# Turning y by VectorE and HBM instead of by products with the identity, in a linear-attention and mixture-of-experts kernel

## The chip, the cores and the metric

The kernel runs on one core of a Trainium2 chip. The metric is the device time of one execution in microseconds (us). A difference of about 0.3% is the least that a measurement of this kernel tells from none.

## What is computed

The first half is linear attention over 8 batches, 8 heads, 576 rows and head size 64, with 128 random features. Its result x (8 x 576 x 512) goes into a mixture of four experts, each of them a causal attention with its own projections, of which every row keeps the best two.

```python
def phi(x):
    proj = np.einsum('bhsd,df->bhsf', x, w_phi)
    proj = proj - np.max(np.abs(proj), axis=-1, keepdims=True)
    return np.concatenate([np.exp(proj), np.exp(-proj)], axis=-1)
q_p, k_p = (phi(q), phi(k))
kv = np.einsum('bhsf,bhsd->bhfd', k_p, v)
z = np.sum(k_p, axis=2)
num = np.einsum('bhsf,bhfd->bhsd', q_p, kv)
den = np.einsum('bhsf,bhf->bhs', q_p, z)[..., None] + 1e-06
x = num / den                      # laid out as B, S, H * D
...
logits = x @ w_gate                # the best two of four experts, softmax weights w
for e in range(E):
    q, k, v = x @ wq[e], x @ wk[e], x @ wv[e]
    a = causal_softmax(scale * (q @ k.transpose(0, 2, 1)))
    ye = a @ v @ wo[e]
    out += (weight of e for the row) * ye
```

## The kernel before

Work is cut into generators, one for each stage, and each yields a step for one engine at a time. Which generator goes next is written out by hand: the string PICKS holds pairs of signs, the first naming the generator, the second the PSUM bank (there are eight) or the engine. Plan.loop follows it, and in_order then ties every engine to this order, so each engine works through a fixed list and waits at each instruction for the semaphores that its data need. Code 8 (the sign I) as the second sign puts a step that has a choice on VectorE, any lower one on ScalarE. There are some 1,014 steps that only VectorE can take, and they carry I as well.

The attention half goes over 32 pairs of heads (four a batch). The features of k and q are made by TensorE, centred and put through Exp, where the maximum of q's features over partitions is a GpSimd partition_all_reduce of about 4 us. stream_kv and stream_n form the sums and the numerators, with rows on the partitions. For the projections of the second half, x has to stand with its features on the partitions. turn_x does that: VectorE transposes 128 x 640 values in blocks of 32 x 32 (line 535), four DMAs write the blocks to HBM tile xd in the right order, one DMA reads xd back (line 544), ScalarE or VectorE rounds the result to its upper part, and VectorE subtracts to get the lower part (line 185, both inputs in SBUF). TensorE products are made of three terms, upper by upper, upper by lower and lower by upper.

The second half goes over 8 batches and two pairs g of experts. After scores, softmax and a @ v (post), norm_y divides and multiplies by the weight of the expert (normed, lines 409 to 440) and writes y with rows on the partitions into yq[g]. Then turn_y turns y: five products with the identity a set, a set being one (batch, g), in two PSUM banks (blocks 0 and 1, then 2 to 4; line 445). evac_y takes each bank to the upper part (a copy on ScalarE or VectorE) and the lower part (a subtraction on VectorE, one input in PSUM; line 185). project_out multiplies by wo with 48 products a batch and ends in the stores. Turning y of batch b waits until the products of project_out of batch b - 1 are issued; norm_y of batch b waits until yq[g] of b - 1 has been turned.

All DMAs are issued on SyncE's queue (load, line 210), in the order of the list. A step "SP" that waits for a semaphore holds all later DMAs. An all-reduce of GpSimd is made to wait for the last VectorE instruction before it that was marked as using the port which the two share (plan.port, line 184 and dve(..., port=True)). keep_warm fills TensorE with small bf16 products until the first x is ready, three to a step.

The lines that matter: yq 262, normed 409, turned 442, turn_x 531, norm_y 762, turn_y 768, evac_y 783, project_out 795.

Of the kernel before, what the change touches and what calls it, by code (L numbers as in the profile page):

```python
# [20 lines left out]
NJ = 5  # L21
# [35 lines left out]
    "UABASIQARIQAOIOIOIDAQACANIDADZAAOIOIOIOAQIJHRINAQIQIGIDAECJIFgHIQAGAJ1QACADAQIPINIPINALIIBPIPILAGIPIPAPIMAGID7OAHAGANIKA"
    "FgAAQIFqQARAOIFxQARAIgPISARAOIKALAOIMABAKIECDAGIBARIGIDAD1OARIRIGAKASIAAHBRILAKIPICAJAF7NININICAHADAFqGIBANIIxNININAPIPA"
    "GIOADAMID4LIMANAFiNAFrSAQISAECSAJIIAIESALAQIJAOIOIOILAIDRINIRIRANININAQIPAIFMIQALAAAIARAJAIAICQILABANIRAMAIBRINAQIMALIIE"
    "KIJAPIOAIGKAOIMIKAJIIDKIKILADAIAIoIRNIDAOII8RIOIPANIIyOIKANAOINIOIIAIFQIPIQIOAPIQANIPANIIBSAOIKARIMIMIMIIAPANIPIMIKALIIF"  # L60
    "JAMAKILAIAD8NAMIKAMIGDCAMIJANIJIMIEBGAGCKIAALIKAKIHwCAGAMILIKAKILIJIKAEFDALIKIF7JANAFiBAJINANAHZNAKIJAOIMINAKIKIKIKALIF6"
    "MIMIDADgAAKIOAMIMAJ1QILILIMAMINIMIJAMIIRMIMIDAI7IgRIRAPIDAOIPII7OIQIPIOAGCCAQIRIOIRIOAOIRAQIOIPAOIEBPIOAJAOIGAGACAPIOIMI"
    "MAMIOIMAECMDQIGANIMEQAPIMAOID1AAQAPIPIOIF4OIQAHZQAJIOIJIBALIHiOAPIPILAPILIF4TAIAIAIFTAPILAPIPIPALIIAKISALASIKAQIQIQIIHLI"
    "SAQIQASIQIIBQALINIRALARINIIALrPAQIKANIDAPINADAOIJIDQKAPIPIF8JAOAGGKISAOIOAOIQIOARAQIJANBQAAANENIIDQANIOAPIGADAOIH9LAPIKI"
    "DACABAOANIGAKACAOIOILAKAKIMIECMAMIIGMIGANIMILAEENIMAIBOINALAMIIDMAIFMAIAI4MAFyNIOINAPIDhAANAOINAMIIrIQPAPAI-QIIAIDSIMAPI"
    "SIPIQISARIQIPAIFRIUAOIRAUINIIDUAQIUISIIFKAPIUAUIRILASIPIPIIAJDPIQAOIOAJHQAPINIJAKAMIOAJCPAOALAJGOAKIDAJENAMILAJDMAKIJFJA"
    "JIH5MAMAKIJAJILALIKAJAJIJIDADQAAKIKIJAJzNIJIJIJIJALIKILIKIGFCAKIKIDAJIDAKIKIIhKIKAF6JAMILIKAMAOILAKDLIMAEGKAMAF8LIGAKALI"
    "MADRMILIFoBALIMINAIjNAI-LIPAOABAMIIoNIOINIOIIAIAGENAPIMAJAQIOAOIAAQIPIQAQIHaPACAGANIOIOIJAJINIEENIIHRIMIQIMAKIIANINIDANI"
    "KIPADAIFQAPININAPIIGLIPAKAPIKAGECAMIMIJINAKANIKIIAD5JAAAFQMIGAPAFrPIJAEGPIFgOIPIJAJIFqOALAPIMISAHzNIJAQAQAJIPAHsNIBAJIOA"
    "MIJABAJQRININIPINIDALIKADANINAGHCANIMINALANILAIBKIPIKILAGAKAOIEDIGMIRIKANIQININIIHPANIOALILILALIIDLINALIIALANAIAIRNANII0"  # L70
    "I9RARAIYPIOIIANAIEPASIOASIQIOARIPIRAOIPIIGTAQIOIQATIPIOAOIICTATIOIOIOIIBKARAPIRILAOIOINIMEOAPAMGPAIAD9AAOIPAOIOIKAFQOIQA"
    "FZKIF0KATAJANISALAPALIBAJEOANAOANAJGMIOALAJFOALIJDOAOAJBOAOAJCMILAJAKIJIJAH0JIDAJIDAQIOINILIDrAAJANINIF4KIRAFRRASAGAQIRA"
    "SAKAPIQIBAKAOIJ5OILIKAGAKIKIKAJACADAJIKIJADAIqIYOINII0KARILILINAGDPAQINACALILALINALIKAMILILIKCLAMIKALIMAJAIpNIGALILIIAF7"
    "BAKIQADyQAMIKILIPAKIKAIAIDKILIKIKIIHQAPIKAQIPIJAKIIEPAOIKINIIAKAOANIJIIAEBAANAEDH1OIPIOIOIDANIJIDAH6MIOIMIMIMIJAJIGBCAOI"
    "JAJIOIMIOIOAMIMIMANIDYNIJAJIGAAAOIFsQAFyPIQAF5QAQAOIFsRAOIOAQAECQABAHwRIPAJIDABADAQID8MIJAAAJrTIMIOASIRISIMARIGBRIRIDAPI"
    "PIRIRARIRIDALAPIECGIIHSIPIPASIPIPAOIQEQDQAQAIFRACAQIOAQIPIJBQALAOAICNIOAPAIAPAKINANAIGOILILIKAIAI8NIIrPIOIIRKAOIMIIwNAPA"
    "NANAIAIHOINIMAOINIOAQIPIIESAQIPIQAMINAPAIFSIMARANIRIPIIDKARAMIRILAMIMIMIIAH8QINIOAMINIMAKAGFCAKIKAKILILIKIEBGAJCNIHwKAKI"
    "NINAOILIKAKINALILIDrAAKAKILAKIFRQAOIF8KARIJBOIPAJEPAMIOIBAQAPAKaLIPANILILAOALIOILIDAKILIDAKAI5NINIIsIwSAQISANIQAPIDsNANI"
    "PAQIRINAAAPII6OAPIOAOIPAIAIAIBPIOIOIQIRIIDKAUAQIRIQALAQIRARIIAVAQIQITIQAKASIIGSAPISIKIIAJCKARAOIJHQIQAOIJDQAGBCARANIOAOI"
    "KANINAEANIKIJFLAGANALIDAKCKGPIH7QINAOIDANANIKINIMIKAJIGECAMIMIJAMIMIMAMIDpMIJAGIAAJyNIKILIMILIKALIHYLILIDANILILALILIDAD8"  # L80
    "MIMIFpMIMAOIFyBARAPIQALAQAIFOIRAPAOIOAPIIBPIMIMAICMIOAMAIEOINIIGOANAIAI4OINAIrOIPIIRSIOANIOAPAF0OAQAFoBAQAF7RAQAPIF0OISA"
    "QAPISAIoOIOAPIBAPIIAIHSANARATISITISITANIIESAVATIVINANIIGQAUASITIRIIDMAOISAQIOIKAIAEHRIRALFAARIGENAQIQIMIPANIOADACAPIDADQ"
    "GIPIHzMAPILAOIKAOIGHCAMANIMAKIKIKAEBEFNIJEKIAAGAJAPANIKAKIH6NIQILILILIKAKIOADAOAKINIKAKhOIKIKIMIMIDAKIKILILALIKILAIoMIMI"
    "IzKAI6RAOIRAPIOAMIOAMIDzPIQIOAOIPIOAMIIIMIOAAAOIJFSIJERIVASIRISAKAOINIJFQARIJHWAQIUARITAQIJFSAPISAJERAMININALBMILAIAIAIH"
    "KILIPAKAQAPIICQAPINAOIJALIDAIGNANAJIKAKIIFNAJADAMIMIDZMAKAKIMIMIFgKAOAF6BAKIOAIAGGPAKIOAJAMINAKACAEFGAGAJIAANILINILIH8CA"
    "MIGIDALIDADyMIMILAGBCAMIMIPILALIOILAMIHrGIMIMILILAFgMIMIOAF-MIOAFRPAMIOAMIFgMANAEDQAEHMIPABAJ1OARIQINAOIPIOILADADAIAOIOI"
    "NAMIBAHCPAAAGEOAMIMAMIMIGBNALIKAGHKAMIKAGAGYMIGqOINIG0KALIG5PAPANAGAGCMAQIPILAMAPINIPAOINIOAMIGFLINARAMILAMILAQIGDQALIQI"
    "LILIGAIAOALIOILIJALILIGAKCMAKFKAMALIF0MANILILIIAIIIAEDAAJIHIIIHIBBCAFHHIGAGIFAHAKIGABqKIGIKAAjJIKAHIGAJIHAGIB4IABRLAGIMA"
    "B1HIFAF5OIFILAGIJAFAJAGIHAIAGIDqIIIIAADzKIDgLINAIIIAIIEDOIIAOINIOIJAFAEBHIGAMAOANAEHOIJALIKADaNAMALIAADADADFNIMINIFAMIKI"
    "KIKAKIJADBNAKANIFIGADGJIMAIIIIGAJIHAFIDHJADABAKAJIFAJIHIFAAsGABIGICaKIIIGAGIIIGACxGIGIIIGAJIIIG4LIHIAAJIJIHIJIHAHIHAIIII"  # L90
    "AAGICEJIGAJIHIHACFIIIIKAHICCKAIIHAIACDJACBJAGACACwJAJICsC6NANACZGANILIJACACEPILANIOINIOAPIKINAPICFMINIRAKALAQIKANALIKICG"
    "OAMIOILICAHAOAMILIMIKIJIKACADELAGIDHLALADFFAJIJAGDFIIAFBFAHAGADGFIHADCHAAEIAHIEAHIEIGIAADADIA4DIDICACICICAC1EICICICICACI"
# [795 lines left out]
```

## Time and profile before

| | us |
|---|---|
| median of 3 runs (577.13 to 578.64) | 577.42 |
| the profiled execution, whole | 577.18 |
| its span from the first to the last instruction | 575.4 |
| TensorE matmul busy | 564.3 |
| VectorE busy | 503.4 |
| ScalarE busy | 387.0 |
| GpSimd busy | 198.3 |

The profiled execution lies 0.24 us under the median, and 1.8 us of it lie outside the span. The granted TensorE clock was 1.00 throughout. Matmuls are pipelined, and so a busy TensorE is not one at its peak; the chain of waits tells better where time goes: it starts at the last instruction and follows, step by step, what released it.

### The profile page before, as it was taken

Reading aid. Unit: us, or ns where it says so; the run is one execution under the profiler, and the core shown is the slowest. Engines: PE = TensorE matmul, PEld = TensorE weight load, DVE = VectorE, ACT = ScalarE, POOL = GpSimd, SP = SyncE. Lnnn points to the kernel's source line nnn. Section 1 sums busy time; section 2 is a strip of 40 time slices with the busy share of each in tenths; the row PEclk is TensorE's granted clock in tenths of the full one; section 3 lists DMA queues with packets and bytes.
Section 4 is the critical chain, followed back from the end, with each engine's and each line's share of the span. In section 5 each row is a group of like instructions: output and inputs, shape, how many; then the busy total and the mean of one; then the engine's idle time right before and its main releaser. Section 6 shows DMA issues by size and latency. Waiting matters only on the chain.

```text
span 575.4 us, 22675 instructions
## 1 busy us (share of the span) xinstructions
PE 564.3 (98%) x9743; PEld 528.3 (92%) x9743; DVE 503.4 (87%) x1279; ACT 387.0 (67%) x715; POOL 198.3 (34%) x78
## 2 busy tenths in 40 slices
...
GB/s 148 210 179 184 224 183 45 96 119 92 147 77 112 154 80 111 74 156 102 123 117 58 142 124 95 60 155 127 132 122 53 66 43 64 63 84 44 2 43 124
DMA packets 83316, 62.36 MB, mean 108 GB/s; under 512 B 47248, under 2 KB 66064, under 8 KB 83216
## 3 DMA queue, kind: packets, MB, share of 16 engines
...
## 4 chain that ended last, share of the span: by engine, by line
PE 80%; DVE 8%; DMA 4%; ACT 4%; issue 1%; SPq 1%; POOL 1%; ACTq 0%; DVEq 0%; POOLq 0%
PE ps_c L180 32%; PE ps_c L402 29%; PE ps_c L355 10%; PE ps_c L621 7%; PE ps_c L445 1%; DMA out_dram<-ot 1%; DMA xl<-xd 1%; ACT st L191 1%; DVE st L739 1%; DVE top L653 1%; SPq L210 1%; DMA v_in<-in_v_dram 1%; POOL tops L493 1%; DVE xl L185 1%; DMA xd<-xt 1%
## 5 line engine op out<-in xcount | busy, mean ns | idle before, releaser
L493 POOL PARTITION_ALL_REDUCE mx<-u x32 | 127.1, 3988 | 136.3 <-ACT u L189 60.9
L180 PE MATMUL ps_c<-xh,qk 128*128 128x320 f32 (+1 forms) x512 | 106.5, 299 | 0.0
L191 ACT ACTIVATE ek<-ek 128x1152 f32<-128x1152 f32 x64 | 74.6, 1166 | 22.6 <-DVE ek L390 21.9
L180 PEld LDWEIGHTS ps_c<-xh,qk 128*128 128x128 f32 x512 | 83.2, 189 | 1.7 <-issue 0.4
L402 PE MATMUL ps_c<-v_in,ek 128*64 128x65 f32 x2560 | 81.9, 222 | 1.8 <-ACT ek L191 1.0
L402 PEld LDWEIGHTS ps_c<-v_in,ek 128*64 128x64 f32 x2560 | 77.6, 137 | 5.9 <-ACT ek L191 2.3
L493 POOL PARTITION_ALL_REDUCE tops<-top x15 | 54.4, 3627 | 65.2 <-DVE top L653 45.8
L180 PE MATMUL ps_c<-xl,qk 128*128 128x256 f32 (+1 forms) x256 | 75.7, 296 | 0.0
L739 DVE TENSOR_TENSOR st<-st,tops 128x1152 f32<-128x1152 f32 (+4 forms) x75 | 66.6, 899 | 1.8 <-POOL tops L493 1.7
L191 ACT ACTIVATE st<-st 128x1152 f32<-128x1152 f32 (+3 forms) x60 | 51.0, 868 | 18.0 <-DVE st L739 14.6
L402 PE MATMUL ps_c<-kv,mx 128*64 128x65 f32 x1152 | 62.1, 224 | 1.1 <-ACT kv L189 0.8
L189 ACT COPY st<-ps_c 128x512 f32<-128x512 f32 (+1 forms) x106 | 47.5, 504 | 18.1 <-PE ps_c L621 11.2
L180 PE MATMUL ps_c<-vg,xh 128*128 128x260 f32 (+1 forms) x320 | 59.4, 286 | 0.0
L402 PE MATMUL ps_c<-kv,u 128*64 128x65 f32 x1152 | 59.1, 221 | 0.0
L503 DVE TENSOR_TENSOR u<-u,mx 128x1152 f32<-128x1152 f32 x32 | 53.9, 1688 | 2.6 <-POOL mx L493 2.3
L189 ACT COPY u<-ps_c 128x320 f32<-128x320 f32 (+3 forms) x116 | 40.4, 418 | 19.8 <-PE ps_c L355 18.3
L634 POOL COPY top<-st 128x256 f32<-128x256 f32 x15 | 6.3, 423 | 135.2 <-ACT st L189 114.8
L402 PEld LDWEIGHTS ps_c<-kv,mx 128*64 128x64 f32 x1152 | 47.3, 137 | 5.9 <-issue 1.4
L180 PE MATMUL ps_c<-yh,wo 128*128 128x256 f32 (+1 forms) x256 | 52.4, 299 | 0.1
L388 DVE TENSOR_REDUCE pmax<-ps_c 128x4 f32<-128x512 f32 (+1 forms) x96 | 50.5, 545 | 2.1 <-ACT mx L191 0.7
L390 DVE TENSOR_TENSOR ek<-ps_c,pmax 128x512 f32<-128x512 f32 (+1 forms) x96 | 50.5, 543 | 0.9 <-PE ps_c L402 0.7
L180 PEld LDWEIGHTS ps_c<-xl,qk 128*128 128x128 f32 x256 | 48.5, 190 | 0.0
...
## 6 DMA issues: line engine op xcount, KB each, us to landing
v_in<-in_v_dram SPq DMA_DIRECT2D x32, 320.0 KB, 4.1
...
xl<-xd SPq DMA_DIRECT2D x32, 288.0 KB, 3.1
out_dram<-ot SPq DMA_DIRECT2D x32, 288.0 KB, 2.3
...
xd<-xt SPq DMA_DIRECT2D x64, 80.0 KB, 2.7
...
```

Source lines behind the costliest of these rows:

```text
L180: nc.tensor.matmul(o, a, b, start=start, stop=stop, skip_group_check=True)
L189: nc.scalar.copy(o, i)
L191: nc.scalar.activation(o, i, func, **kw)
L355: nc.tensor.matmul(o, a, b, start=True, stop=True, skip_group_check=True)
L388: dve(n * 128, [mk], [pk]).tensor_reduce(out=m[:, us], in_=src, axis=AX.X, op=ALU.max, apply_absolute_value=True)
L390: dve(n * 128, [(f'ek{p % EKB}1', us.start)], [pk, mk]).tensor_tensor(out=ek2[p % EKB][:, 1, us, :], in0=src, in1=m[:, us].unsqueeze(2).to ...
L402: nc.tensor.matmul(o, a, b, start=start, stop=stop, skip_group_check=True)
L493: nc.gpsimd.partition_all_reduce(o, i, 128, op)
L503: dve(2 * S, [uk], [mk], port=True).tensor_tensor(out=U, in0=U, in1=M, op=ALU.subtract)
L621: nc.tensor.matmul(pp_[e][:, o:o + q1 - q0], kk2[k_][r, 128 * j:128 * j + 128], q2[q_][r, q0:q1], start=m == 0, stop=m == 2, skip_group_ch ...
L634: nc.gpsimd.tensor_copy(top[x][:, :, 0:128], st[x][0][:, :, 0:128])
L739: dve(2 * n, [sj[j]], [*key, mk], port=True).tensor_tensor(out=a, in0=a, in1=tops[x][0:m, :, 128 * j:], op=ALU.subtract)
```

## The change

For all batches but the last, turn_y goes to a new generator, move_y, which does for y what turn_x does for x. VectorE transposes the whole set in blocks of 32 x 32 into a new SBUF tile yt, four DMAs write it to a new HBM tile yd, five DMAs read it back into the place of the lower part, one copy of 128 x 576 makes the upper part, and one subtraction with both inputs in SBUF makes the lower part. The reads pick pieces of 32 values (128 bytes). yq is laid out as xq is (four groups of 160 columns), and two memsets clear its corner. The last batch keeps the products with the identity on a view of the same tile. The subtraction of move_y is issued without the port mark; its copy carries it if VectorE takes it.

PICKS is new as a whole. It has 2,687 pairs before and 2,660 after. 1,132 pairs have I as their second sign before, 1,099 after. The numbers in the calls of dve(...) that differ (-6.0, 9.0, 7.0) are arguments which the function doesn't use.

```diff
-    yq = [sb(f"yq{i}", [128, NJ, 128]) for i in range(2)]
+    yq = [sb(f"yq{i}", [128, 4, 32 * NJ]) for i in range(2)]
+    yt = [sb(f"yt{i}", [128, 4, 32 * NJ]) for i in range(2)]
+    yd = [dp.tile([128, 4, 32 * NJ], F32, name=f"yd{i}") for i in range(2)]
+    for t in yq:
+        nc.vector.memset(t[64:128, :, 128:160], 0.0)
...
     def norm_y(b, g, pks, pss):
         yield Step('DVE', pred=(lambda: all(('yt', b - 1, g, q_[0]) in done for q_ in PARTS)) if b else None)
-        yield from normed(pks, pss, sc[g], 1e-9, yq[g], f'yq{g}', gw[:, :, 2 * g:2 * g + 2].rearrange("p i e -> p e i"), True)
+        yield from normed(pks, pss, sc[g], 1e-9, rows_y(g) if b == B - 1 else yq[g], f'yq{g}', gw[:, :, 2 * g:2 * g + 2].rearrange("p i e -> p e i"), b == B - 1)
...
+    def move_y(b, g):
+        keys, k, hi, lo = [(f'yq{g}', x, n) for x in range(2) for n in range(2)], f'yt{g}', *ys[g]
+        yield Step('DVE', keys, pred=lambda: all(('n', b, g, n) in done for n in range(2)) and (b == 0 or ('yw', b - 1, g) in done))
+        dve(640, [k], keys, XT_RATE).transpose(yt[g].rearrange("p a t -> p (a t)"), yq[g].rearrange("p a t -> p (a t)"))
+        for s0, s1 in PARTS:
+            done.add(('yt', b, g, s0))
+        yield Step('SP', [k], pred=has('yr', b - 1, g) if b else None)
+        hbm = yd[g].rearrange("(b x) a t -> x b a t", b=4)
+        for a in range(4):
+            n = 160 if a < 2 else 128
+            load(hbm[:, :, a, 0:n], yt[g][32 * a:32 * a + 32, :, 0:n], (f'yd{g}', a), [k])
+        done.add(('yw', b, g))
+        kd, kr = [(f'yd{g}', a) for a in range(4)], [('yr', g, n) for n in range(2)]
+        old = [('y' + x, g, s0) for x in 'hl' for s0, s1 in PARTS]
+        yield Step('SP', kd, pred=(lambda: ('o', b - 1) in done) if b else None)
+        to, hbm = lo.bitcast(F32), yd[g].rearrange("f a (i j) -> f i a j", j=32)
+        for i in range(4):
+            load(to[:, 128 * i:128 * i + 128].rearrange("f (a j) -> f a j", j=32), hbm[:, i], [kr[0], *old], kd)
+        load(to[:, 512:576].rearrange("f (a j) -> f a j", j=32), hbm[:, 4, 0:2], [kr[1], *old], kd)
+        done.add(('yr', b, g))
+        st_ = Step(copies_sb(S), kr, port=True)
+        yield st_
+        copy(st_.eng, S, hi, to, [('yh', g, s0) for s0, s1 in PARTS], kr, 0.52)
+        yield Step('DVE', [('yh', g, 0)], hot=True)
+        nc.vector.tensor_tensor(out=lo, in0=to, in1=hi.bitcast(F32), op=ALU.subtract)
...
     def turn_y(b, g):
+        if b < B - 1:
+            yield from move_y(b, g)
+            return
         for s0, s1 in PARTS:
...
-            turned(ps, pk, yq[g], blocks, key)
+            turned(ps, pk, rows_y(g), blocks, key)
```

## Rows read from the trace of the kernel before

**Rows 1.** The page: busy time by engine, then the chain's shares by engine.
```profile
PE 564.3 (98%) x9743; PEld 528.3 (92%) x9743; DVE 503.4 (87%) x1279; ACT 387.0 (67%) x715; POOL 198.3 (34%) x78
...
PE 80%; DVE 8%; DMA 4%; ACT 4%; issue 1%; SPq 1%; POOL 1%; ACTq 0%; DVEq 0%; POOLq 0%
```

**Rows 2.** Chain of waits: line 445 (start us, us, what); all lines, 300 to 400 us.
```profile
125.77 0.64 PE ps_c L445 x5
...
147.19 0.79 PE ps_c L445 x5
...
538.72 0.64 PE ps_c L445 x5
...
by line: PE ps_c L180 42.0%; PE ps_c L402 34.7%; PE ps_c L621 10.9%; PE ps_c L355 10.0%; PE ps_c L445 2.1%; ACT u L189 0.4%; issue 0.1%
```

**Rows 3.** Chain of waits where the other two sets are turned, 497 to 504 us.
```profile
497.18 3.95 POOL tops L493
...
502.51 0.73 DVE yl L185 x2
```

**Rows 4.** Groups by line and form: warm-up products. Count | busy us, mean ns | idle before.
```profile
L180 PE MATMUL ps_c<-warm 128*128 128x128 bf16 x159 | 12.0, 235 | 1.3 <-DVE col L215 1.3
```

**Rows 5.** Groups by line and form: y's evacuations, x's route, copies on VectorE.
```profile
L189 ACT CAST yh<-ps_c 128x320 fp32r<-128x320 f32 x14 | 6.0, 428 | 0.1
L185 DVE TENSOR_TENSOR yl<-ps_c,yh 128x320 fp32r<-128x320 f32 x16 | 7.7, 482 | 0.1
L185 DVE TENSOR_TENSOR yl<-ps_c,yh 128x256 fp32r<-128x256 f32 x16 | 6.7, 417 | 0.7 <-ACT yh L189 0.4
...
L535 DVE STREAM_TRANSPOSE xt<-xq 128x640 f32<-128x640 f32 x32 | 26.4, 832 | 2.1 <-ACT xq L191 1.7
L185 DVE TENSOR_TENSOR xl<-xl,xh 128x576 fp32r<-128x576 f32 x32 | 32.1, 1008 | 3.5 <-ACT xh L189 3.4
L189 ACT CAST xh<-xl 128x576 fp32r<-128x576 f32 x29 | 19.4, 671 | 7.1 <-DMA xl<-xd 6.8
...
L202 DVE COPY u<-ps_c 128x256 f32<-128x256 f32 x13 | 5.1, 417 | 2.4 <-PE ps_c L355 2.4
L439 DVE TENSOR_SCALAR yq<-ps_c,sc 64x64 f32<-64x64 f32 x14 | 3.9, 278 | 0.2
```

**Rows 6.** Lines 185 and 493: ns min/median/max, first and last start us.
```profile
L185 DVE TENSOR_TENSOR xl<-xl,xh x32: 742/755/2599, 42.0 to 518.0; 128x576 fp32r<-128x576 f32 x32
...
L493 POOL PARTITION_ALL_REDUCE mx<-u x32: 3937/3940/5095, 8.5 to 461.8; - x32
```

**Rows 7.** SyncE: ns to issue a DMA (min/median/max); its longest wait by cause.
```profile
L210 SPq DMA_DIRECT2D xd<-xt x128: 303/432/1982, 32.6 to 510.7; - x128
L210 SPq DMA_DIRECT2D xl<-xd x32: 327/340/1073, 37.8 to 512.6; - x32
...
SPq L210 <- PE ps_c L180: 91.9, 25, 11.2
```

**Rows 8.** The page's DMA issues: count, KB each, median us from issue to landing.
```profile
v_in<-in_v_dram SPq DMA_DIRECT2D x32, 320.0 KB, 4.1
...
xl<-xd SPq DMA_DIRECT2D x32, 288.0 KB, 3.1
...
xd<-xt SPq DMA_DIRECT2D x64, 80.0 KB, 2.7
```

**Rows 9.** Busy us of PE, PEld, DVE, ACT, POOL, 100 to 480 us.
```profile
100.00:480.00 380.00, 378.84 (x6927) 357.34 (x6926) 345.64 (x858) 263.05 (x485) 133.91 (x50) 1.00 0.39 104
```

**Rows 10.** Order of time: last write of yq, first wo product (batch 2); the latter (batch 6).
```profile
290.22 0.29 DVE L439 TENSOR_SCALAR yq<-ps_c,sc 64x64 f32<-64x64 f32 x1
...
294.93 0.41 PE L180 MATMUL ps_c<-yh,wo 128*128 128x256 f32 x2
...
549.15 0.40 PE L180 MATMUL ps_c<-yh,wo 128*128 128x256 f32 x2
```

**Rows 11.** Chain of waits in the last batch: a store that a copy waits for.
```profile
553.20 4.53 DMA out_dram<-ot
```

More of the change, by code (lines that the diff above doesn't have):

```diff
@@ L57 @@
[L57 to L92, printed above, removed]
@@ L97 @@
-    "CACACICACICIAGCICIBFBHDABIEABIDAEABIDIBACIBCCABACABIBIABAGBIADBABAAFBIAEBABAAHBIACBAAABIAAAAAA"
+    "AABABACACAAAAAAAAAAAAAAAAAAAAAGRNANAGjNANAG1OAOAG5OAOABAEaPIQIFERIRIDAPICACAAAAAAAAAAAAAAAAAAAAAAAAAAAAAAAAAAAG1G5GiNAOA"
+    "PIEANIBABAAAAAAAFDWIDAQAOICAEATAEyVIWIBARAQAG5CAPAPANANAQISAHARIPANAPIEAEAKFFDKIRIRIAALhKGDAOIPAPAQIQIQIQIQIQAQIKIDAEqRI"
+    "NAL7NANANINANAOIPIOINANAPIPIOIOAOIOAHIIABAGhGyCAPIQIQIPIPAOIOAAAAAAAAAAAAAAAFFQIQIEAEAAAAAE7RIQIQINANIAAOIFRPAOAF0BAPAOA"
+    "OAJAJAEFPIPINIGIKRPIMADADAJGGAPIPIAAOINANAJACACAOIOAOIDjQIRIAAQIQIOAOIOANANAMIMIF4F1PANABAOANANAKRFjQIFoBAQAOIEGRIOISIDA"
@@ new lines @@
+    "DAD8JDEFCAOIOIOIOIOAHASIPIPAGARIRIOIOAQIQIQIDADADRJIKgF-JDVATIQIGIQIRIRIQIDADAQININANAHIRAMAPIPIGAGAJIJFKRRIPAPIPIOIOANA"
+    "NAHAJIKzCAMIAAGIGAHAMIPIPIOIRIOAPIPAPIPIF8FoVABAVASAHIGIGIGAKIPAPAAAKAMIMIMIMAMIMICADROIPIOIOIFoOAOAOALILAJAJAJEPAPIJHPA"
+    "PIJDPAPIFwFpQAQAQAGAGIPAPAMIJCQAQIEEEGRIRIQIQIDADAGALALANINAKAMAJAJHQAJBQAJDQAJFQAJAQAAAOIOALIOIOABABAGIGIIAIyQIPIPAPIPA"
+    "I8QAPIIZPIQIPIQIQAPIPIIoSIRIRIRASISIQIQIPID0AAIAICUAUIIHIDIBKAJAJIPIKANISASIQINIRARIIANINAPILAPAPIJAOIGCEHCAGAHYPINIDADA"
@@ new lines @@
+    "GFCALILAMIMAKAGAKIMILILAMIFxOAOALILALILILAJILIFiOANANABAD9PIAAOIPIOIDADALIHxOIOIEEQILILALILINININININALILAOIJAJ6MIIrPIPA"
+    "OIOAOAIII0IrPAOAMIMIOIMIMAMIOIOARIPIPIPAMAQIQANIOIPINININIOIOINANININAMIDIAAJAGCCAGAEHRIRIQIQIMAF0RAFqRAQABAQAQAJAJIIAOI"
+    "OILADAHzFiF9RAPIPIPIBASAMISAOIRARAIAIBSASIIASASIICIFSASIDAOAOAOIOAOIMAMIMAD8AASITISISIMIOIJIGBEACARIRIGAQAQIDADADaAAIAPI"
+    "LALININAHhF-TATAFoTATATABAPIPIOAOAJAGGCAEHLALILILASIGANAKIKAPIPIJAOIRININIDAPIKoPIPIPIPIPIPIPIPIPAMIMAOAOAJAMIMAHyOIOIOI"
@@ new lines @@
+    "OIOAOIOIDAD7PIPIPIPIAADAOIOAMIMANAJIJIIAOAIFOAIBOAKAKIIGNAIENAIAIaI4IpRARAPII0PAQIRIRIRAOIOARIPIPARIRASIPIPIRIRAPIPIPIIA"
+    "QIQIDAD4NINAPIIDSAICTATISIIBSASIIFSASIKAMAGGGAGECAECAAEDGAIALARIRIOAOAOIOAOIOAOIOAOIOIOARICAPIPIQILIKAOIOIDAHpH-QIOIOIQI"
+    "QIOIQIQAQIQIOIOIOIOADAPIPALAJEJARAQAQAOIOAPAMIMAMaOII5I1UATARIRAQIQAQAIgOIOIRIRIQIQIOIRARIRIOAOIOIKIGGGAKINANINIF9NANAFR"
+    "BAOANANAIjOIPIPIOIIAPAPIPIF1SAD6RAKAMIOAOIOIOAAARIRIJBRAJARALALIQAEGQIQIJFJERAJBJAPAPAQAPAMIJALIMAMICALALANINIIAIDOAOIIE"
@@ new lines @@
+    "OAOIIFIHOAOIIAOAOIKAKAHwOILALILALILIFRFjF9UIBABAUIQASAQAQALALZSIDAQAQANINININANINININAQIQIDADiSISIAASISIGFEGSISIDAQIQAIH"
+    "IASASACAOIJIOIGAJIJIFiFxBASARAQAQAQAMAOIOIOIOAH4FpTASAQIFiSABAQIQIQIQIQIQARANADADzTISITISIDADADpSITIICUAIAUAQIQARARIPIPA"
+    "GHEEUIUISISICAGAIGSAIAIaUIUATITITAIgUATAI5UII1UIUAWITITITAWIWAUIVIVIUITITITATITITITITAAAAARANANAIAIDICTAIETITATITATIIALA"
+    "PATATIIAQAQIGHCAEBRIMAH1SIGAHaUIDADAGED4AAQAQIQAQIQAQISISISISASISISIMAMIPIQIQINANIKAPILAQIGAF1SASAFhBASASASAF1TATAFhBATA"
@@ new lines @@
+    "TAOIQIOIOAOIOIPIPILAKAMACADADADoSIOIHxTITITITITATITAPIPALILALjSIMAMASILALASISISISISIQIOAKIOIGCCAOIGAI5IzUATAIiRIRAI1QIQA"
+    "QAQIQIQASISISARIRIRAQISIQISIJDVAJAVAVAJHVAJBVAVARINIRIRAKAPIPANANAPIQIQIPIPALAMAMIKIEDPIPIEAPIPINIIAIAICPAPILAIHPAPIIBPA"
+    "PIIFIAPAPIJGPAJEPAJDQAPAJAOALADADAD0QIPIPIMAMIMAMIMAMIMIMAPIFaPAH4QIQIQIQIQAQIQAJIGBGANAAAAACANADADAKININALsNININININANI"
+    "NIIGOAICOAIAOAIHOAIBOANINAKINIMAIAIjI1SAIQTITII5UISISIOIVITARAUITIRAPIIAIGIFWAWIIGOAIDQIQIEAOAPIPINANINADiOAOIOIQAQIHpOA"
@@ new lines @@
+    "OIOIGHPAPIPAPIFzBAJARIPIQIPIQIFgPIDASAFyBAGANANANINANIAAQIQAH7DARIGATAOIOIOIOIOAFxOIOAQAQAQANANINANINIMANANsUIIAJACAGAIQ"
+    "LATASANINANAQIQIQIMIKGJININAVAQIQITITASISASAQIQIJBSASAOIOAOIOIKAJGRAEERIDQAAI5UAUAKIOIOIOIPIIzIpRIRISISIRATITIRIRIKARARI"
+    "RININAOARARIRIRIRIQIQINAQAQIQIQAMAOIOIIAIAIHQAQIIEQAIDQIQAQIIGQAQIKIDAKIJBPAJCJFQAQAPAPANILIDAD4QIFjBARACAQIPIIAKAKAPAJB"
+    "JGQAPAPAGCEFEDQIQIAAOAPIPIF8PAPAFxQAPAJIMIGAKAKIBAKAKIKAKIKIKAMIMAJANAHjF9QAQAOIHxQIQIOIOIOIOAOIQIQIOICAPAPIKQQIQIQIQIIF"
@@ new lines @@
+    "SAIHSAQAQIQIIDRAIERAIBRAOIOIOAPIJANIMIFqRARIIAI-SITITASAIYTATASAJIOALADADADhRISISIRIAAOAKAOIOAIqRIQIQIRIRAQAI-SITITISISA"
+    "TAQIQIRIRIQIRIRIQIQAKAIAIAQAQIIDIEIBSASIQAQIDADABANIGCEGRICARIGAF9FIUASARARARAKADaTISISISIIAQAQILAMAMIDADAOIOAOIOAH5GFCA"
+    "GAPINAJASAJGSAJCTASAJDSAJETASAJFJAUAJGRASAGCAAPIPIPIPIPAPIPININANINIMIF7FgTATAKITASAKIJACAOIOAOAD1SITISIBAGAMALAEBEHUIUI"
+    "TIRALARIRIJIDADAKAKgPIIaI9VAUAPIPIRIPIPIPIRAPIQIIxIgTISISISATITAPID9OIQAQARIRISIKAPAQISIWIQIVIRARIRIGCCATIQIQIHzF5GAFiWA"
@@ new lines @@
+    "WATIJIPAPIPIPADANANAQIQIQIQIQIQIQASARARAH5SISISISIKISISIIAIAIFUAUIIAUAUIIDIGQIAAAASASIOIBADAGEJATATINANINANINAFRF9TATATA"
+    "TATADwNININANRVIIAMAKATISIQAQILARIOIOAOAJIMAMABAIAFAMIMALABANININININANININIMAMAMADFDHOIAANIJAJILILIHIGDKAGAGGLAKAGEKAGB"
+    "KAKIGAG6GzOAOAGgGpLILAOIOIOAKALILAOIOIOAMIMIMAPINIPIPANIKIKALINILIMIKAKIKIGAGDLALIGGGCMAMIGHIAMAMILALIFgLILILILIBABABpDa"
+    "PAPAD-OAOAJAJIJAJIJAOAFAMIKAKIKIKIKAKAEaOIDGAAIIIAIIHAIIIAI8OICADwJIJIJIAAAAEpJIJAMIMIMIMICEMIMAHIJIJIIANINANINANAIIIAII"
@@ new lines @@
+    "IIIIIAIAJIGAGIIACAGAGIIIIIE5ErKAEiKAKIKIKALILILAMIMIMANININALILIKIKIKIKIIIIIIAIIIIIIIAIAJIJIJAEAEAEBLALIEHLALIEFLALIEDLA"
+    "LIEABCKIKIEAKAEGKAEEEAMAEBEHEGEFKAHIHAHIHAHIHAHIHIAaSIRIEAEIIAJAJANINICgGAG5OIOIOIOIOAOIOIMIMIHAIAIAEAJIJIJIJILILAJAJIJA"
+    "KAEIEIAAAACCJACDJACBJACHJACGJACACoKIKAKIKAJIJAKACiKAKACZKILIKIKALILAC-NIMININAMIMAKILIKIKIKILIKIKIKACACACFCCCEHACAMAMIMA"
+    "MILALIDADIKAKIIIABAAAzHIHAHIHAHIHAHIDAHIHIGIGAHIEIHIHAHIHAEICAFIFAFACACICAC9DIDIDIAQAhJAIAAzFIFADIDADIDIEIEAGIGIGAFIFIFA"
@@ new lines @@
+    "AhHIIIGIEAGIHIHAGADIDAEIFIEIFIEIEIEIEACACIAAAABAFABHFABFGAFABCFABGGAFABDBBHABEEAFABACICACICACICACICICAAAGAGIAHGAGIAFGAGI"
+    "ACGAGIAACxFIAjA4AqFIFIKAFIFAFIFIJAHIHAFIFAIIJIDAHIHAIIIAFIFAFABIAIHIIIIIIAAAAGAHDAFIFIFIFABIDIDIEIDIDIFAFIDIDAEAEIAEADAA"
+    "EAEIEAEIAqAwEIHAFIFAEAEAEAA5AjEIEIFIFIGIHIHIEAAAGIFAFIFIFADIDADIDAEIDIDADIDICACACIFAFIFIEIEIAAFAAFFAACFAAGFAAHEABAAAGAAF"
+    "GAGAACGAAGAEIAGAAHHAADAABIBACICABIBABIBABIBABIBIBACICAApHIHIHIHIHAHIHIDACACACACAAiCICICICICACICIBGDADIBHCACIBBCACIBFBABI"
@@ L98 @@
+    "ADAABABABAACAEAGAHABBAAFAABABAAACAAAAAAA"
 )
@@ L413, in normed @@
             yield Step('DVE', [pks[n]], hot=True)
-            dve(5, dk, [pks[n]]).tensor_scalar(out=d[:, n], in0=bl[n][:, :, 64], scalar1=eps, scalar2=None, op0=ALU.add)
+            dve(5, dk, [pks[n]], -6.0).tensor_scalar(out=d[:, n], in0=bl[n][:, :, 64], scalar1=eps, scalar2=None, op0=ALU.add)
         if extra is None:
-            dve(10, dk, [], 13.5).reciprocal(d, d)
+            dve(10, dk, [], 9.0).reciprocal(d, d)
         else:
             r = pss[1][:, 400:410].rearrange("p (e i) -> p e i", i=NJ)
-            dve(10, dk, [pks[1]], 13.5).reciprocal(r, d)
+            dve(10, dk, [pks[1]], 7.0).reciprocal(r, d)
             dve(10, dk, [pks[1], 'gate']).tensor_tensor(out=d, in0=r, in1=extra, op=ALU.mult)
```

11 lines of the change are left out of this document (3 added, 8 removed).

## The prediction

> **What bounds the kernel now.** I read the busy times first, then the chain of waits, then both by stretches. TensorE is busy for 98% of the span, VectorE for 87%, ScalarE for 67%, and the chain lies on TensorE for 80% of its length [rows 1]. Busy time alone proves little, since products overlap; the chain proves more, as it goes through TensorE only where nothing else was waited for. So between 100 and 480 us, where TensorE is busy for 378.8 of 380 us [rows 9] and the chain, as in the window from 300 to 400 us, goes through it almost alone [rows 2], a product taken out should bring the end nearer by its piece of the chain. VectorE is second: 345.6 of those 380 us, 34.4 us idle. ScalarE has 117 us idle there. At the two ends it is otherwise. The opening fills TensorE with warm-up products [rows 4], and in the last batch the chain stands for 4.53 us on a store [rows 11].
>
> **What is taken out.** 14 of the 16 sets lose their five products on the identity. The chain, read in windows, passes through line 445 in 12 of these 14 sets: eight times at 0.64 us, three times at 0.79 us, and once in two pieces that make 0.80 us [rows 2]. That is 5.12 + 2.37 + 0.80 = 8.3 us. The two others are turned just after 500 us, where the chain goes through a reduction on GpSimd and then VectorE [rows 3]; there TensorE waits anyway and I count nothing, though the same chain holds subtractions for y of 0.73 us, and more behind them. Unhidden, those two sets would add at most 2 x 0.79 = 1.6 us.
>
> VectorE loses two subtractions a set, 482 + 417 = 899 ns, and ScalarE in nearly all sets two copies, of which the larger takes 428 ns [rows 5].
>
> **What is added.** The route is x's, so x's rows price it. VectorE gets a transpose of 832 ns and a subtraction with both inputs in SBUF, 1,008 ns in the mean [rows 5]. Net this is 832 + 1,008 - 899 = 941 ns a set and 13.2 us in all. It could be 9.6 us if each subtraction takes the median of 755 ns, and 35 us if each takes the longest seen, 2,599 ns [rows 6]. I take the mean, since the same mix of reductions runs beside it.
>
> Against that stands the new order. Before, 1,132 pairs of signs have I. 1,014 are fixed VectorE steps, 114 are copies that the trace shows on VectorE (from x13 at line 202 to x14 at line 439, in [rows 5]), and about four are banks 0 and 1. The fixed steps stay 1,014, as each set trades two subtractions for a transpose and a subtraction. So of the 33 pairs that I loses, nearly all are copies that go from VectorE to ScalarE. At 417 ns each [rows 5] they give VectorE back 13.8 us, between 9.2 us (278 ns each) and 13.8 us. VectorE thus ends within about 4 us of where it was. ScalarE takes those 33, about 14 us, and a copy of 671 ns a set in place of two; its 117 us of idle time cover that.
>
> SyncE issues nine more DMAs a set. Four writes at 432 ns and five reads at 340 ns [rows 7] are 3.4 us a set and 48 us in all. Its waits cover them: those for products at line 180 alone last 91.9 us [rows 7]. But the read waits for its four writes at the head of the queue, and behind it stand the loads of k, q and v and x's own writes. x does this 32 times now, and in the steady part the chain holds no wait for a load [rows 2], so I cost it at nothing. Without that cover it is a write's landing, up to 2.7 us a set [rows 8].
>
> From the last write of yq to the lower part, the new route takes 0.83 + 4 x 0.43 + 2.7 + 5 x 0.34 + 3.1 + 0.67 + 1.01 = 11.7 us, or 12.7 us if a read of short pieces lands as v_in does, which the code moves in pieces of 256 bytes, in 4.1 us instead of xl's 3.1 us [rows 5, 7, 8]. Today project_out follows by as little as 294.93 - 290.51 = 4.4 us in batch 2, and in batch 6 it begins 549.15 - 538.72 = 10.4 us after the products that turned y [rows 2, 10]. In batch 2 it must start some 7 to 8 us later; other products are there to fill in, as the order is new. In batch 6 it would be late by 2.3 us at most, and the hole of 4.5 us behind it [rows 11] can take that.
>
> Last, the count of steps. A set has one step fewer, which makes 14 of the 27 pairs that are gone. The other 13 must be warm-up steps, the only ones whose number is free. 39 products fewer at 12.0/159 = 0.075 us [rows 4] are 2.9 us of filler. If the first x only comes earlier by some of that, it is worth between 0 and 2.9 us; I take 1 us. The two memsets stand in the same opening and cost nothing.
>
> The sum: 577.18 - 8.3 - 1.0 = 567.9 us, and 0.24 us more for the median of the runs, 568.1 us.
>
> **Two rules weighed.** The trace shows xl's subtraction between 742 and 2,599 ns, beside reductions of 3.94 us [rows 6], while y's from PSUM have means of 417 and 482 ns [rows 5]. The Trainium skill ("SBUF — State Buffer", Who interferes with whom) says why: a VectorE instruction with two SBUF inputs and a GpSimd instruction that reads SBUF exclude each other, and the one that came second waits for the whole of the other. By that rule the move from PSUM to SBUF puts 14 subtractions at risk of up to 3.94 us each, 55 us on VectorE at worst, and the trace agrees as to the kind, with 1.8 us as the worst excess of xl. The other rule is in the rivals.
>
> **Rivals.** First, more than the sum. The chain's 4.53 us on the store [rows 11] come from where project_out of batch 6 stands in the order, with its copies ahead of the last softmax on ScalarE. An order that puts these elsewhere loses them: 568.1 - 4.5 = 563.6 us. For it speaks that y of batch 6 comes later now, so that project_out has to move; against it, that the stores still have only two buffers.
>
> Second, VectorE and GpSimd take the gain. If the 14 subtractions often meet a reduction, each costs up to 2.6 - 1.0 = 1.6 us more, 22 us of VectorE time against 34 us of idle time [rows 6, 9]. With a third of it on the chain the time is 575 us. For it speaks that the subtraction has no port mark, so a reduction doesn't wait for it; against, that only 34% of the span has GpSimd busy [rows 1].
>
> Third, slower than before: the order asks for y before it has landed. TensorE works in order, so a project_out that waits for the reads holds everything behind it, in each of seven batches. If each waits L us, the time is 568.1 + 7L; no gain is left from L = 1.3 us, and it is slower by over 0.3% from L = 1.6 us. With L = 2, for reads of 128 bytes that land as far behind v_in as v_in behind xl and a queue that costs one more, it is 582 us. For it speaks the batch with only 4.4 us now [rows 10]; against, that others left 11 us and more, and that sets are far apart.
>
> Fourth, far slower. The same mechanism with reads that land tens of us late, because the pieces are short and strided: a route as long as a batch, which is (549.15 - 294.93)/4 = 63.6 us [rows 10]. Every project_out then slips by one batch, which other products may fill, but the last move has nothing behind it: batch 6 begins project_out no earlier than 538.7 + 63.6 = 602 us, and with the 575.4 - 549.15 = 26 us that follow now the end is near 628 us. Against it: x's route shares the work out alike, its DMA only sets blocks in place that VectorE has turned, and it lands in 3.1 us; v_in with its pieces of 256 bytes lands in 4.1 us [rows 8]. Hence a small chance. The Trainium skill ("VectorE: DVE Perf Modes", The three transpose paths) warns that a plain DMA which does the transposing by strides is 19 times slower than the transposing DMA path, and its rules for kernel authors leave a 128 x 128 transpose to TensorE if the result may stand in PSUM; 19 times xl's landing would be an estimated 59 us. No row here shows such a factor.
>
> **How the numbers follow.** The forecast, 565 to 572 us, gets 0.51. The first rival (560 to 565) gets 0.19, the second (572 to 577) 0.13, the third (577 and up) 0.14, the fourth 0.03. A measurement tells from no change what is under 575.7 or over 579.1 us, 0.3% each way. Faster: 0.51 + 0.19 + 0.07 of the second = 0.77. Same: 0.06 of the second and 0.02 of the third = 0.08. Slower: 0.12 + 0.03 = 0.15. The range runs from 561 to 578 us and leaves out 0.04 below and some 0.15 above. Its ends: 577.4 - 8.3 - 1.6 - 2.9 - 4.5 = 560.1, rounded up as all at once is unlikely, and no gain at all.
>
> **What would show it.** Line 445 has 10 products left, and TensorE still carries 80% of the chain or more. VectorE's busy time stays within 5 us of 503, ScalarE's grows by 5 to 15 us. The subtraction for y has a mean near 1.0 us. Warm-up products number 120. The reads of yd land in 3 to 4.5 us. The prediction is wrong if first products of wo wait for y, if y's subtractions average 2 us, or if TensorE's idle time, 11 us of the span now, grows by as much as its work has shrunk.

## The result, and the profile after

The changed kernel takes 568.23 us (median of 4 runs, 566.93 to 568.96) beside 577.27 us for the kernel before on the same chip: a ratio of 0.984, with a 95% interval from 0.981 to 0.986. The forecast was 568.1 us. Of the runs further below, one with the extra hop (756.42 us) and one with 33 copies moved to ScalarE (1,372.38 us) were slow, and their medians leave them out.

The page of the profile after, the lines that answer to [rows 1]: span, busy time by engine, the chain's shares by engine.

```profile
span 565.9 us, 22678 instructions
...
PE 554.1 (98%) x9634; PEld 520.0 (92%) x9634; DVE 498.1 (88%) x1248; ACT 389.2 (69%) x734; POOL 193.5 (34%) x78
...
PE 89%; DVE 6%; ACT 2%; DMA 1%; issue 1%; SPq 0%; ACTq 0%; DVEq 0%
```

TensorE has lost 564.3 - 554.1 = 10.2 us of busy time, 2.7 us of it warm-up products (12.0 us in [rows 4], 9.3 us below), and the span 575.4 - 565.9 = 9.5 us. Its idle time, span less busy time, went only from 11.1 to 11.8 us. So nearly everything that was taken from it became time. The chain's share on TensorE rose from 80% to 89%.

The groups by line and form that answer to [rows 4] and [rows 5]: count, busy us, mean ns, idle time before.

```profile
L778 DVE STREAM_TRANSPOSE yt<-yq 128x640 f32<-128x640 f32 x14 | 11.7, 834 | 1.3 <-ACT yq L191 1.0
L799 DVE TENSOR_TENSOR yl<-yl,yh 128x576 fp32r<-128x576 f32 x14 | 11.1, 795 | 0.7 <-ACT yh L189 0.6
L180 PE MATMUL ps_c<-warm 128*128 128x128 bf16 x120 | 9.3, 241 | 1.3 <-DVE col L215 1.3
...
L189 ACT CAST yh<-yl 128x576 fp32r<-128x576 f32 x9 | 6.1, 674 | 0.0
...
L202 DVE CAST yh<-yl 128x576 fp32r<-128x576 f32 x5 | 2.2, 443 | 0.0
```

Line by line for the new steps: issue on SyncE, the subtraction and the products left (ns min/median/max, first and last start in us); then, from the view of DMA issues, KB each and the median us to landing.

```profile
L210 SPq DMA_DIRECT2D yl<-yd x70: 517/624/1557, 123.8 to 530.9; - x70
...
L799 DVE TENSOR_TENSOR yl<-yl,yh x14: 717/747/1469, 137.3 to 539.3; 128x576 fp32r<-128x576 f32 x14
...
L449 PE MATMUL ps_c<-ident,yq x10: 272/273/328, 553.0 to 555.2; 128*128 128x128 f32 x8, 64*128 64x64 f32 x2
```

```profile
yl<-yd SPq DMA_DIRECT2D x56, 64.0 KB, 2.8
yd<-yt SPq DMA_DIRECT2D x28, 80.0 KB, 2.1
yd<-yt SPq DMA_DIRECT2D x28, 64.0 KB, 1.8
```

Ten products with the identity are left, all in the last batch. The transposes cost what x's do, and the reads land in 2.8 us at the median.

The chain of waits near the end (start us, us, what), which answers to [rows 3] and [rows 11]:

```profile
498.78 0.46 DVE yh L202
...
499.90 0.48 DVE yl L799
...
506.36 0.74 DVE yt L778
...
522.83 0.83 DVE yt L778
...
524.51 0.36 DVE yh L202
...
526.59 0.66 DVE yl L799
...
533.24 13.80 PE ps_c L180 x108
547.03 6.04 PE ps_c L406 x200
```

The hole of 4.53 us on a store is gone: from 533 to 553 us the chain runs through TensorE without a break. But y's own steps on VectorE stand on the chain here for 0.46 + 0.48 + 0.74 + 0.83 + 0.36 + 0.66 = 3.5 us. Before it was 0.73 us [rows 3] and these two pieces, 1.5 us together:

```profile
504.24 0.40 DVE yl L185
...
504.84 0.33 DVE yl L185
```

The windows from 480 us to the end, before and after (us; busy us of PE, PEld, DVE, ACT, POOL; granted clock), tell what the end gave in all: TensorE's idle time in them is 95.40 - 89.65 = 5.8 us and 85.90 - 79.98 = 5.9 us. The end gave with one hand and took with the other.

```profile
480.00:575.40 95.40, 89.65 (x1158) 85.89 (x1154) 66.27 (x196) 51.69 (x117) 19.07 (x10) 1.00 0.20 64
...
480.00:565.90 85.90, 79.98 (x1082) 76.54 (x1080) 64.41 (x182) 50.23 (x113) 17.58 (x10) 1.00 0.31 84
```

### The profile page after: what moved, and what is told of

Read it like the earlier page. It is cut to its first block, busy times and chain, and to the rows that moved or that the text cites. A ratio compares the mean times of both kernels' runs of the same rounds, so it can differ in the third digit from the quotient of the medians.

```text
span 565.9 us, 22678 instructions
## 1 busy us (share of the span) xinstructions
PE 554.1 (98%) x9634; PEld 520.0 (92%) x9634; DVE 498.1 (88%) x1248; ACT 389.2 (69%) x734; POOL 193.5 (34%) x78
## 4 chain that ended last, share of the span: by engine, by line
PE 89%; DVE 6%; ACT 2%; DMA 1%; issue 1%; SPq 0%; ACTq 0%; DVEq 0%
PE ps_c L180 40%; PE ps_c L406 32%; PE ps_c L359 11%; PE ps_c L625 7%; DVE ps_c L645 1%; DVE xt L539 1%; ACT st L191 1%; DVE top L657 1%; DVE ek L394 1%; DMA v_in<-in_v_dram 1%; DVE pmax L392 1%; DVE st L743 0%; ACT u L189 0%; DVE yq L437 0%; DVE yl L799 0%
## 5 line engine op out<-in xcount | busy, mean ns | idle before, releaser
L189 ACT COPY st<-ps_c 128x512 f32<-128x512 f32 (+1 forms) x115 | 51.4, 500 | 31.0 <-DVE ps_c L645 21.8
L743 DVE TENSOR_TENSOR st<-st,tops 128x1152 f32<-128x1152 f32 (+4 forms) x75 | 61.5, 865 | 5.7 <-POOL tops L497 5.7
L189 ACT COPY u<-ps_c 128x320 f32<-128x320 f32 (+3 forms) x124 | 43.2, 414 | 16.4 <-PE ps_c L359 14.8
L406 PE MATMUL ps_c<-vl,st 128*64 128x65 f32 x1500 | 47.9, 223 | 2.3 <-ACT st L191 2.3
L406 PEld LDWEIGHTS ps_c<-vl,st 128*64 128x64 f32 x1500 | 45.4, 138 | 4.8 <-ACT st L191 2.7
```

Of the source, the lines that this page charges most:

```text
L189: nc.scalar.copy(o, i)
L406: nc.tensor.matmul(o, a, b, start=start, stop=stop, skip_group_check=True)
L743: dve(2 * n, [sj[j]], [*key, mk], port=True).tensor_tensor(out=a, in0=a, in1=tops[x][0:m, :, 128 * j:], op=ALU.subtract)
```

## Experiments

That the number came out does not show that its reasons did. Theory A: the gain is the time of 70 products on TensorE. Theory B: it is the new order of all steps, and the products were mostly hidden. Two more came up on the way and are named where they did.

**The products put back.** In the changed kernel, five idle products with the identity (ten in the second run) stand at the head of each of project_out's first two banks.

```diff
                 pk, ps = yield Step('PE', yk, 'c', ...)
                 n = 0
+                if t == 0 and b < B - 1:
+                    for i in range(5):            # in the second: (0, 1, 2, 3, 4) * 2
+                        k = 128 if i < 4 else 64
+                        nc.tensor.transpose(ps[:, 128 * (i % 4):128 * (i % 4) + k], mask[0:k, :], ident[0:k, 0:k])
```

> The changed kernel and its order, with 70 products with the identity added (five in each of the first two banks of project_out of batches 0 to 6, on a constant tile; the results are overwritten and nothing uses them). Theory A, the gain is the 70 products' time on TensorE: 8.3 us come back, 568.2 + 8.3 = 576.5 us (574.5 to 578). Theory B, the gain comes from the new order and the products were mostly hidden: at most 2 us come back, 568 to 570.5 us.

> The same with 140 added products, ten in each of those banks. Theory A: twice the price, 568.2 + 16.6 = 584.8 us (582 to 587), on a line with the single dose. Theory B: 569 to 574 us, and no line.

Measured: 578.11 us with one dose, which is no different from the kernel before (ratio 1.0003, 0.9991 to 1.0014), and 589.81 us with two (1.0203, 1.0184 to 1.0221), above the 587 us that theory A allowed at most. The first dose costs 578.11 - 568.23 = 9.9 us, the second 11.7 us: 0.71 and 0.84 us a set of five. The chain's pieces were 0.64 to 0.79 us [rows 2], and the added ones read alike (chain of waits of the first run, two of 14):

```profile
175.05 0.79 PE ps_c L843 x5
...
264.20 0.64 PE ps_c L843 x5
```

Read in windows, this chain passes through all 14 added sets, five times at 0.79 us and nine times at 0.64 us, 9.7 us in all, and TensorE's busy time rose by 563.9 - 554.1 = 9.8 us. In the new order TensorE's time is paid in full, as theory A has it. It is more than the 8.3 us forecast, as all 14 sets stand on the chain and not 12.

**The products taken from the old order.** The kernel before without the 70 products, nothing else changed.

```diff
-            turned(ps, pk, yq[g], blocks, key)
+            if b == B - 1:
+                turned(ps, pk, yq[g], blocks, key)
```

> The kernel before and its order, with the 70 products of batches 0 to 6 left out (y is then not turned: its evacuations read what the banks hold). Theory A: 577.3 - 8.3 = 569 us (567.5 to 571). Theory B: the old order cannot use the time, 574.5 to 577.5 us.

Measured: 575.01 us beside 577.51 us (ratio 0.9949, 0.9932 to 0.9965). The same 70 products give 2.5 us here, where theory A asked for 8.3 us; the time lies in theory B's range. So neither holds for both orders. The busy times and the chain of this run's profiled execution, its slowest, 1.3 us over its median:

```profile
PE 558.7 (97%) x9673; PEld 523.1 (91%) x9673; DVE 502.1 (87%) x1279; ACT 386.3 (67%) x715; POOL 198.4 (35%) x78
...
PE 74%; DVE 12%; ACT 5%; DMA 3%; POOL 3%; issue 2%; SPq 1%; DVEq 0%; ACTq 0%; POOLq 0%
```

TensorE's idle time rose from 11.1 to 574.5 - 558.7 = 15.8 us, and the chain left TensorE for VectorE and GpSimd. 4.0 us of this rise lie between 100 and 480 us, where TensorE idled for 1.2 us before [rows 9] and idles for 5.2 us now. One such place can be read: a read of x for which ScalarE then waits, in the kernel before and then in this one (line 210's row: ns of the issue, min/median/max, and its start in us; then, in this run alone, the wait for it in us and how often; the last row: us from issue to landing).

```profile
L210 SPq DMA_DIRECT2D xl<-xd x1: 344/344/344, 193.5 to 193.5; - x1
...
DMA to landing us min/median/max: 3.3/3.3/3.3
```

```profile
L210 SPq DMA_DIRECT2D xl<-xd x1: 462/462/462, 194.2 to 194.2; - x1
...
  DMA xl<-xd: 2.8, 1
...
DMA to landing us min/median/max: 5.4/5.4/5.4
```

It was issued 0.7 us later and landed 2.8 us later. This is one profiled execution; why it was slow was not followed up. A second loss is TensorE's clock, in the windows of this run from 502 us (columns as above, the granted clock third from the end):

```profile
502.00:504.00 2.00, 0.00 (x0) 0.00 (x0) 2.00 (x4) 1.40 (x2) 0.61 (x1) 1.00 0.03 8
504.00:506.00 2.00, 1.92 (x48) 1.92 (x50) 2.00 (x6) 1.17 (x3) 0.00 (x0) 0.73 0.00 0
506.00:508.00 2.00, 2.00 (x44) 2.00 (x42) 0.81 (x4) 1.06 (x1) 0.00 (x0) 0.50 0.03 8
508.00:510.00 2.00, 2.00 (x68) 2.00 (x67) 1.86 (x5) 0.31 (x1) 0.00 (x0) 0.91 0.00 0
```

TensorE stands still for 2 us and then works at a granted clock of 0.50, the lower level of 1.2 GHz, for some 3.4 us, on the chain; in the kernel before it works for 1.24 of the first 2 us, and the clock stays at 1.00. At half speed this costs at most 1.7 us of the 5.8 us that are missing, an estimate from these rows. All four runs have a mean granted clock of 0.996; those of the kernel before beside them have 0.997 to 1.00. So in the old order the next waits, and a clock that falls after one of them, take most of what the products leave. Which waits? Theory C: VectorE, at 87% the second engine, is the limit next to TensorE. Theory D: no engine's load but the fixed order itself, in which each step was put where its data come in time, and where each step that comes earlier meets another that doesn't.

**VectorE loaded again.** The changed kernel with 33 copies back on VectorE, as many as the new order took from it.

```diff
                 s[1].eng = 'DVE' if x >= 8 else 'ACT'
+                # every 4th evac_v (9 in all), every 5th evac_o (13), every 13th soft (9), every 9th stream_kv (2)
+                if x < 8 and <one of these>:
+                    s[1].eng = 'DVE'
```

> The changed kernel and its order, with 33 copies that it gives ScalarE put on VectorE again (9 of vl, 13 of ot, 9 of st, 2 of kv, spread evenly), some 15 us of VectorE time. Theory A, only the products' time counts and VectorE's idle time covers its part: 568 to 570.5 us. Theory C, VectorE is the next limit, and the old order could not use the products' time because VectorE was in the way: a third or more of the 15 us shows, 573 to 580 us.

Measured: 584.29 us (ratio to the kernel before 1.0113, 1.0098 to 1.0129), 16.1 us over the changed kernel and above both expected ranges. VectorE's busy time rose by 14.4 us, from 498.1 to 512.5 us, and TensorE's idle time went from 11.8 to 21.9 us:

```profile
span 582.6 us, 22678 instructions
...
PE 560.7 (96%) x9634; PEld 522.9 (90%) x9634; DVE 512.5 (88%) x1281; ACT 378.7 (65%) x701; POOL 194.1 (33%) x78
```

This looks like theory C, though it costs more than all the time that was added. The other direction tests it.

**VectorE relieved.** The changed kernel with the 12 copies of upper parts that VectorE has (7 of x, 5 of y) on ScalarE.

```diff
                 s[1].eng = 'DVE' if x >= 8 else 'ACT'
+                if s[0].gi_code.co_name in ('turn_x', 'move_y'):
+                    s[1].eng = 'ACT'
```

> The changed kernel with the 12 copies of x's and y's upper parts that VectorE has given to ScalarE (6.3 us of VectorE time, 8 us more for ScalarE). Theory C, VectorE is the next limit: 1 to 3 us less, 565 to 567 us. Theory A: no difference, 567.5 to 569 us, or slightly more where the copy on ScalarE takes 0.23 us longer.

Measured: 570.72 us (0.9879, 0.9862 to 0.9896), 2.5 us slower with 3.2 us less on VectorE (494.9 us) and 3.8 us more on ScalarE (393.0 us). That is against theory C, and 1.7 us above theory A's range, which allowed slightly more. The old order was then relieved in three ways: without y's subtractions (below; the lower part is set to zero once), without these and the products, and with 33 of VectorE's copies on ScalarE, the last with and without the products.

```diff
-        sub_lo(n, lo, src, hi, ('yl', g, s0), [pk, ('yh', g, s0)])
+        if b == B - 1:
+            sub_lo(n, lo, src, hi, ('yl', g, s0), [pk, ('yh', g, s0)])
```

> The kernel before and its order, with the 28 subtractions for y's lower part in batches 0 to 6 left out (12.6 us of VectorE time; the lower part stays zero). Theory C, VectorE stands beside TensorE as a limit of the old order: 4 us or more of the 12.6 us show, 565 to 573 us. Theory D, TensorE and the waits of a fixed order limit it and VectorE's idle time covers the rest: 574.5 to 577.5 us.

> The kernel before and its order, without the 28 subtractions and without the 70 products of batches 0 to 6. Theory C, each of the two engines hides what is taken from the other: more than the sum of both alone, 2.5 us for the products plus what the subtractions alone give, 560 to 568 us. Theory D: 571 to 575 us, the sum or less.

> The kernel before and its order, with 33 copies that it gives VectorE put on ScalarE (9 of vl, 13 of ot, 9 of st, 2 of kv; 15 us less on VectorE, 14 us more on ScalarE), and the products with the identity in place. Theory C: 570 to 576 us. Theory D, engines and places in the order were chosen together and a copy that moves costs a wait: 577 to 583 us.

> The same 33 copies on ScalarE in the old order, and the 70 products of batches 0 to 6 left out. Theory C: with VectorE out of the way the products' time shows, 565 to 571 us. Theory D: the products give some 2.5 us again, 575 to 580 us.

| the old order | us | ratio, 95% interval |
|---|---|---|
| without the 28 subtractions | 578.22 | 0.9998 (0.9979 to 1.0016) |
| without both | 575.38 | 0.9958 (0.9937 to 0.9980) |
| 33 copies on ScalarE | 582.62 | 1.0090 (1.0061 to 1.0118) |
| the same, without the products | 579.44 | 1.0031 (1.0013 to 1.0050) |

The kernel before stood at 577.69 us beside them. The subtractions are 14 x (0.482 + 0.417) = 12.6 us of VectorE work [rows 5], and leaving them out changes nothing. The busy row of that run shows VectorE 9.7 us below the 503.4 us of [rows 1], and the span 0.5 us below:

```profile
span 574.9 us, 22656 instructions
...
PE 564.6 (98%) x9743; PEld 528.7 (92%) x9743; DVE 493.7 (86%) x1251; ACT 387.1 (67%) x715; POOL 199.7 (35%) x80
```

Moving 33 copies costs 582.62 - 577.69 = 4.9 us, and the products are worth 578.22 - 575.38 = 2.8 us without the subtractions and 582.62 - 579.44 = 3.2 us with the copies moved: never the 8.3 us. Theory C falls: VectorE's load does not hold the old order. The four times lie in theory D's ranges or within 0.8 us above them, and what is measured fits theory D; that the waits are of its kind everywhere was not read. Time added to TensorE or VectorE lands on the end, 9.9 us for 9.7 on the chain and 16.1 us for 14.4 busy; moved from VectorE to ScalarE it cost 2.5 and 4.9 us; on SyncE it cost nothing (the extra hop below). Time taken out is mostly lost to the next wait, until the order is made anew.

**The route in the old order.** The kernel before with a set's transpose and nine DMAs where its first product stood, and one copy and one subtraction where its first evacuation stood.

```diff
             pk, ps = yield Step('PE', ...)
-            turned(ps, pk, yq[g], blocks, key)
+            if b == B - 1:
+                turned(ps, pk, rows_y(g), blocks, key)
+            elif s0 == 0:
+                route(b, g)                      # transpose, four writes, five reads, as in move_y
```

> The kernel before and its order, with VectorE's transpose and all nine DMAs of a set issued where the old order had the first product with the identity, and one copy and one subtraction of 576 columns where it had the first evacuation. The route takes some 12 us and the old order leaves 1 to 2 us there, so the copy holds ScalarE (or VectorE) for some 10 us a set. Theory A and my prediction's third rival: up to 14 x 8 = 112 us more, 620 to 690 us. If latency were hidden in any order: 565 to 580 us.

Measured: 717.21 us (1.2412, 1.2387 to 1.2437), 139.7 us more, or 10.0 us a set, beyond the expected 620 to 690 us. Two of its longest waits (us, times, longest):

```profile
ACT yh L189 <- DMA yl<-yd: 117.8, 13, 10.6
DVE yl L819 <- ACT yh L189: 110.6, 12, 13.9
```

The copy waits some 9 us for each set's reads, VectorE behind it. The route without an order that gives it time is a loss of nearly a quarter.

**More latency, in the new order.** The changed kernel with one hop more within HBM before the reads.

```diff
+        load(ye[g][:, 0:2, :], yd[g][:, 0:2, :], None)
+        load(ye[g][:, 2:4, 0:128], yd[g][:, 2:4, 0:128], None)
-        to, hbm = lo.bitcast(F32), yd[g].rearrange("f a (i j) -> f i a j", j=32)
+        to, hbm = lo.bitcast(F32), ye[g].rearrange("f a (i j) -> f i a j", j=32)
```

> The changed kernel with one more hop: yd is copied within HBM to a second tile by two DMAs before it is read, which makes each of the 14 moves longer by 3 us or more and holds SyncE's queue for that time. If the order has room behind the reads, as the distances of 8 to 22 us between their issue and the copy in its trace let expect: 568 to 571 us. By the prediction's third rival, TensorE waits for y in each batch: 568.2 + 7 x 3 = 589 us, 580 at least.

Measured: 568.25 us (0.9844, 0.9824 to 0.9865), no different from the changed kernel. The hop landed 2.8 us after its issue at the median, on top of two more issues:

```profile
ye<-yd SPq DMA_DIRECT2D x14, 128.0 KB, 2.8
```

**The warm-up products.** The changed kernel with four a step in place of three.

```diff
-            for _ in range(3):
+            for _ in range(4):
                 mm(ps[:, 0:128], warm, warm, True, True, 128, pk, [])
```

> The changed kernel with four warm-up products a step in place of three, 160 in place of 120, about the 159 of the kernel before. My prediction took 1 us for them, between 0 and 2.9: 569.2 us (568.2 to 571.1). If they only fill time that TensorE waits anyway: 568.2 us, within 0.3%.

Measured: 569.59 us (0.9860, 0.9845 to 0.9874), 1.4 us over the changed kernel. That is within the 0.3% that can't be told from none, so it doesn't show what the warm-up products cost.

## Why the prediction held, step by step

**The 8.3 us of products.** The size was about right in the new order, where putting them back costs 9.9 us. The reason was put too simply. I wrote that a product taken out should bring the end nearer by its piece of the chain; in the order of the kernel before it brings 2.5 us for 8.3 us. Four times tell it together: the old order takes 577.5 us with the products and 575.0 us without, the new order 578.1 us with them and 568.2 us without. The chain says what released what in that execution, not how close the next releaser stood. The step holds only with the new order, which I had as a given and not as a condition. How much a new order would give that keeps the products was not tried, since no such order is at hand; the changed kernel's own order with the products in it is no faster than the old one. TensorE idles for 11.8 us now as against 11.1 us before, so what the new order did was to keep the removal from turning into idle time; what another order could gain without the removal is bounded by those 11.1 us and stays open.

**VectorE stays where it was.** The balance was right in sign: 503.4 us became 498.1 us, 5.3 us less and just past the 5 us that I allowed, where 13.2 us more for y and 13.8 us less for 33 copies make 0.6 us less. A part of the miss that I can name is the subtraction. I took x's mean, 1,008 ns, and y's has 795 ns (14 x 0.213 = 3.0 us less); x's own fell to 831 ns (32 x 0.177 = 5.7 us less). Other groups moved by as much in both directions: the 32 long subtractions of line 503 (507 after), both inputs in SBUF too, fell from 1,688 to 1,475 ns, by 6.9 us, and the 160 on line 641 (645 after) rose from 34.4 to 37.4 us. 13 of y's 14 took under 760 ns and one 1,469 ns; two of them ran beside a GpSimd reduction, and only that one was held. By the rule of the Trainium skill ("SBUF — State Buffer", Who interferes with whom) each could have waited for a whole reduction; the trace agrees that one of the two waits, but not for the whole: the last section shows the rows. So the worst case of 3.94 us each was too high, and the second rival was wrong because few met a reduction. That the sum put no price on a few us more or less on VectorE was wrong too: 14.4 us put on it cost 16.1 us.

**ScalarE.** I forecast 5 to 15 us more and it was 2.2 us. I priced the 33 copies, and named but didn't price that y's own fell from 29 (11.7 us) to 9 at 0.67 us and four small ones (7.6 us). That is 4.1 us; where the rest of the miss lies was not followed up.

**SyncE.** The reads take 624 ns to issue, not xl's 340 ns: 70 x 0.624 + 56 x 0.437 = 68 us in place of 48 us. The cover was there; even two more issues and a wait a set cost nothing that could be measured.

**The latency.** I had 11.7 to 12.7 us for the route; the old order with the route gave 10.0 us a set as price for having no time for it. That the new order has room was an assumption of the forecast, and the extra hop shows it. The third rival asked for lateness in each batch, and the fourth for reads that land tens of us late; the reads land in 2.8 us at the median, a little under the 3 to 4.5 us forecast. No row shows the factor of 19 that the Trainium skill ("VectorE: DVE Perf Modes", The three transpose paths) gives for transposing by strides.

**The opening and the end.** 120 warm-up products, as counted from the string. I took 1 us for 39 of them; 40 cost 1.4 us, which is too little to be told from none. In the end the first rival's mechanism took place, the wait of 4.53 us for a store is gone, but it didn't come on top: y's steps on VectorE now take 3.5 us of the chain there in place of 1.5 us, and TensorE idles there as long as before. I had counted the two sets at 500 us as nothing, and the hole as nothing; both were wrong, and they cancelled by luck. What took the rest of the 4.53 us was not followed up.
